# Two-layer decode: a third block of W_q kept, two heads projected earlier, unread MLP products left out

## The chip, the cores and the metric

The kernel runs on one core of a Trainium2 chip. The metric is the device time of one execution in microseconds, as the median of several runs. The same two layers' data are streamed from HBM in every run; nothing is kept between runs.

## What is computed

One token for each of 4 sequences goes through two identical layers, attention and a gated MLP, with the same weights and the same caches in both layers. All arrays are float32.

```
W = 1024                                  # last 1024 of 4096 cache rows, 32 heads of 128
x = x + A(layernorm(x)); x = x + M(layernorm(x))      # and the same once more

A(x): q = x @ wq                          # 640 -> 32 heads * 128
      p = softmax(q . k * 128**-0.5)      # over the last 1024 keys of each head
      return (p . v) @ wo                 # 4096 -> 640
M(x): gate = x @ W_gate; up = x @ W_up    # 640 -> 1728
      return (gate * (gate > 0) * up) @ W_down
```

## The kernel before

The inputs are laid out on the host in three long rows for each of 128 partitions. "heads" holds W_q, the keys, values and W_o of the groups of heads 0 to 6; "kept" holds W_o, W_q, keys and values of the last two groups, K0 and K1 (three and two heads), which layer 0 loads last and layer 1 uses first, so that they are loaded once; "mlp" holds W_gate, W_up and W_down. HEADS (L27) names the groups: six of four heads, then 3, 3 and 2.

Nearly all of SBUF is one tile, `store` (STORE columns), used as a ring, beside a small tile `first_q` (HELD columns), which holds the first HELD columns of "heads" for both layers. Those are the first blocks of W_q of the group 0, 512 columns each; the group has five. `load` (L156) takes the next piece of a list (L108 to L149), cuts it where it would run over live columns or over the ring's end, and issues it on SP's queue. `done` (L200) marks columns as read, frees them and calls `load`. So the moment at which a transfer can be issued is set by the product that read the columns it overwrites, and the order of the transfers by the list. FIRST and FIRST_MLP (L64) say where in the ring layer 0's heads and its MLP begin; at the ring's end the MLP of layer 0 goes on at FRONT = 47360, behind the kept columns. A load waits for one of eight completion semaphores as well, so that about eight are in flight.

An attention layer goes group by group: `query` (L310, products with W_q), `scores` (L338), `softmax`, `turned` (transposes of the probabilities), `values` (L360), `values_turned` (L388, transposes of the outputs `ot`, and VectorE's sums to `oT`) and `project` (L399), which adds a group's outputs times W_o to `y`. The last group's `values` is copied out by VectorE and ScalarE (L377, L378), each half the tile, and in layer 0 the projection of the last two groups follows behind `values_turned` of the last (L440 to L443).

`forward` (L445) is the MLP: four blocks of `gate`, then `down`. In layer 0 it also issues `busy` products (L254): transposes of the identity into `po`, which nothing reads. `busy` does something only while `waits[0]` is true: in every `normalized` (L270), and in layer 0's MLP behind its first gate block. A float32 product stands as two records in the trace, a transpose as one.

Of the kernel before, what the change touches and what calls it, by code (L numbers as in the profile page):

```python
# [13 lines left out]
P = 128  # L14
# [44 lines left out]

HELD = 1024  # L60
STORE = 54944 - HELD
QUARTERS = [STORE // 4, STORE // 2, STORE // 4 * 3, STORE]
FRONT = KEPT * 2 * (D + KV)
FIRST, FIRST_MLP = 10928, 53160  # L64

# [25 lines left out]
def decode_kernel(ctx: ExitStack, tc: tile.TileContext, x, source, sel, out):  # L91
# [162 lines left out]
    def busy(n):  # L254

        if waits[0]:
            for _ in range(n):
                nc.tensor.transpose(po[:, :P], ident, ident)  # L258


    waits = [False]

# [7 lines left out]
    def normalized():  # L270

        ysb, xc, sq = probs[:, :QUARTER], gates[:, :QUARTER], gates[:, QUARTER:2 * QUARTER]
        waits[0] = True
        su = small.tile([P, 1], F32, name="su", bufs=1)
# [123 lines left out]

    def project(layer, g, last=False):  # L399
        o = oT.pop(g)  # L400
        for i, h in enumerate(HEADS[g]):
            for a in range(4):
                nc.tensor.matmul(y[32 * a:32 * a + B], o[:, i], part(layer, "o", h, a * QUARTER, QUARTER),  # L403
                                 start=False, stop=last and h == HEADS[g][-1], tile_position=(0, 32 * a))
            part_done(layer, "o", h, 0, D)

    def attention(layer):
# [13 lines left out]
        for before, g, after, then in zip([None] + gs, gs, gs[1:] + [None], gs[2:] + [None] * 2):  # L421
# [15 lines left out]
            if before is not None and not (layer == 0 and after is None):  # L437
                project(layer, before)
            values(layer, g, after is None)
        values_turned(gs[-1])  # L440
        if layer == 0:
            project(layer, gs[-2])
        project(layer, gs[-1], True)  # L443

    def forward(layer):  # L445
# [4 lines left out]
        def gate(j):  # L450
# [3 lines left out]
            for c in range(KC):  # L454
                for g in range(groups):
                    lo = at + (c * groups + g) * 2 * n
                    nc.tensor.matmul(gus[j][32 * g:32 * g + 32, :2 * n], xT[:, B * c:B * c + 32], get(layer, "mlp", lo, 2 * n),  # L457
                                     start=c == 0, stop=c == KC - 1, tile_position=(0, 32 * g))
                    done(layer, "mlp", lo, 2 * n)
                if j == 2 or j == 1 and c > 2:  # L460
                    busy(2)
                if j == 3 and layer == 0 and c % 2:
                    load(True)
# [23 lines left out]
        def down(j, last=False):  # L487
            for f in range(4 if j < 3 else 1):
# [5 lines left out]
                done(layer, "mlp", lo, D)  # L494
                if not (last and f > 1):
                    busy(1)
            if j == 3:
# [7 lines left out]
        gate(3)  # L505
        waits[0] = layer == 0
        rstd = deviation(ss)
# [75 lines left out]
```

## Time and profile before

| | |
|---|---|
| median of 3 runs | 741.06 us (740.77 to 741.14) |
| the profiled execution's own time | 740.32 us |
| its span | 738.5 us |
| its mean granted TensorE clock | 0.829 |
| read from HBM | 312.24 MB, 423 GB/s over the span |
| PE busy | 453.3 us (61%) |
| DVE, ACT busy | 75.1 us (10%), 47.1 us (6%) |

The page's busy shares are averages over stages. Layer 0's attention runs to about 366 us, its MLP to 399, layer 1's attention to about 711, its MLP to the end. A window of the trace gives busy time, granted clock (1.00 is 2.4 GHz, 0.50 is 1.2 GHz) and the share of the 16 DMA engines that were moving something; the share can read a little over 1, since a packet's time is counted from its own start. The chain of waits is followed back from the last instruction: a transfer stands in it from issue to landing, whether it moves or queues.

### The profile page before, as it was taken

The page shows a single profiled execution, that of the slowest core. Times are in us where ns is not written, and L with a number is a line of the kernel's source. Part 1 is how long each engine was busy: PE and PEld are TensorE (multiplying, and loading weights), DVE is VectorE, ACT ScalarE, POOL GpSimd, SP SyncE. Part 2 cuts the span into 40 slices and gives each one's busy share as a digit, 9 for nine tenths or more (in the row PEclk, how much of TensorE's full clock was granted, in tenths as well). Part 3 has the DMA queues.
Part 4 walks back from the last instruction along what each step waited for, and adds up shares of the span by engine and source line. Part 5 has one row for each costly group of instructions (what it writes and reads, how often), then busy time and mean ns, then how long its engine had stood idle before and what let it go on. Part 6 is the DMA issues. An engine that isn't in the chain of part 4 may idle for free.

```text
span 738.5 us, 8243 instructions
## 1 busy us (share of the span) xinstructions
PE 453.3 (61%) x3749; PEld 143.2 (19%) x3749; DVE 75.1 (10%) x279; ACT 47.1 (6%) x88; POOL 0.2 (0%) x4
## 2 busy tenths in 40 slices
PE   1657366556567636726689898445756545656685
PEld 0111111011122201202333232101211111122242
DVE  1011000010001001101101211001010100001010
ACT  1100000000000000000101110000000000000110
POOL 0000000000000000000000000000000000000000
PEclk9889787867689867969999999867778977668899
DMA  9999999999999999999999999999999999999996
GB/s 393 448 409 439 441 425 428 447 417 431 441 431 424 426 446 411 445 418 420 410 397 394 427 430 427 443 427 446 425 431 423 447 426 425 438 434 427 422 423 281
DMA packets 15738, 312.85 MB, mean 424 GB/s; under 512 B 1748, under 2 KB 2260, under 8 KB 7512
## 3 DMA queue, kind: packets, MB, share of 16 engines
q1 hardware_dynamic: 15552, 312.24, 99.0%
q8 instruction: 29, 0.48, 0.3%
q10 hardware_dynamic: 152, 0.09, 0.0%
q14 instruction: 5, 0.04, 0.0%
HBM read 312.24 MB, written 0.08 MB: 423 GB/s over the span
## 4 chain that ended last, share of the span: by engine, by line
DMA 52%; PE 32%; another core or an unknown queue 14%; issue 1%; DVE 1%; ACT 0%; SPq 0%; DVEq 0%; ACTq 0%
DMA store<-in_heads 30%; PE ps L345 13%; DMA store<-in_mlp 12%; PE po L373 10%; DMA store<-in_kept 10%; PE qp L316 2%; PE pp L358 1%; PE y L403 1%; PE qp L321 1%; PE gu L457 1%; PE qt L333 1%; PE ot L393 0%; PE po L258 0%; PE so L384 0%
## 5 line engine op out<-in xcount | busy, mean ns | idle before, releaser
L345 PE MATMUL ps<-store,qT 128*4 128x512 f32 x1024 | 161.3, 700 | 106.2 <-DMA store<-in_heads 101.1
L373 PE MATMUL po<-store,pT 128*16 128x512 f32 x1024 | 155.9, 720 | 108.0 <-DMA store<-in_heads 97.4
L373 PEld LDWEIGHTS po<-store,pT 128*16 128x16 f32 x1024 | 34.7, 110 | 214.1 <-issue 131.0
L345 PEld LDWEIGHTS ps<-store,qT 128*4 128x4 f32 x1024 | 29.3, 93 | 220.1 <-DMA store<-in_heads 116.1
L349 DVE TENSOR_REDUCE nm<-ps 128x1 f32<-128x1024 f32 x18 | 22.0, 1225 | 243.4 <-PE ps L345 243.4
L353 ACT ACTIVATE probs<-ps,nm 128x1024 f32<-128x1024 f32 x18 | 20.0, 1113 | 353.3 <-DVE nm L349 345.6
L316 PE MATMUL qp<-store,xT 128*32 128x512 f32 (+2 forms) x136 | 23.6, 623 | 24.6 <-DMA store<-in_heads 24.5
L403 PE MATMUL y<-store,oT 128*4 128x160 f32 x512 | 26.0, 332 | 8.8 <-DMA store<-in_heads 7.6
L369 DVE COPY pT<-pp 128x16 f32<-128x16 f32 x128 | 17.1, 168 | 135.6 <-PE po L373 135.6
L457 PE MATMUL gu<-store,xT 128*32 128x256 f32 (+1 forms) x300 | 23.9, 379 | 9.1 <-DMA store<-in_mlp 8.6
L380 ACT COPY gates<-po 128x512 f32<-128x512 f32 x16 | 9.4, 586 | 244.3 <-PE po L373 244.3
L358 PE MATMUL pp<-sel_sb,probs 128*128 128x128 f32 x144 | 20.5, 289 | 0.0
L358 PEld LDWEIGHTS pp<-sel_sb,probs 128*128 128x128 f32 x144 | 18.1, 151 | 0.0
L321 PE MATMUL qp<-store,xT 128*32 128x512 f32 (+4 forms) x48 | 17.5, 512 | 0.0
L326 DVE TENSOR_SCALAR gates<-qp,rstd 128x512 f32<-128x512 f32 (+2 forms) x18 | 12.4, 690 | 49.9 <-PE qp L321 44.5
L386 DVE RECIPROCAL r<-so 128x16 f32<-128x16 f32 x18 | 4.6, 257 | 122.6 <-PE so L384 122.6
L403 PEld LDWEIGHTS y<-store,oT 128*4 128x4 f32 x512 | 13.3, 93 | 19.4 <-DMA store<-in_heads 8.2
L457 PEld LDWEIGHTS gu<-store,xT 128*32 128x32 f32 x300 | 11.0, 115 | 18.1 <-DMA store<-in_mlp 7.4
L492 PE MATMUL y<-store,hT 128*4 128x160 f32 x208 | 11.3, 329 | 3.4 <-DMA store<-in_mlp 3.2
L333 PE MATMUL qt<-sel_sb,gates 128*128 128x128 f32 x64 | 12.3, 316 | 0.0
L393 PE MATMUL ot<-sel_sb,gates 128*128 128x128 f32 x72 | 11.4, 279 | 1.2 <-DVE gates L377 1.2
L333 PEld LDWEIGHTS qt<-sel_sb,gates 128*128 128x128 f32 x64 | 7.6, 155 | 18.6 <-issue 17.3
(62 smaller groups left out, 108.5 us busy)
## 6 DMA issues: line engine op xcount, KB each, us to landing
store<-in_heads SPq DMA_DIRECT2D x18, 6656.0 KB, 54.2
store<-in_heads SPq DMA_DIRECT2D x7, 6912.0 KB, 52.2
store<-in_heads SPq DMA_DIRECT2D x2, 6592.0 KB, 54.6
store<-in_heads SPq DMA_DIRECT2D x2, 5376.0 KB, 65.5
store<-in_mlp SPq DMA_DIRECT2D x16, 640.0 KB, 6.9
store<-in_kept SPq DMA_DIRECT2D x4, 2048.0 KB, 40.4
store<-in_heads SPq DMA_DIRECT2D x3, 2560.0 KB, 20.9
store<-in_heads SPq DMA_DIRECT2D x1, 6896.0 KB, 46.1
```

What stands on the lines that cost most here:

```text
L316: nc.tensor.matmul(qp[g][32 * c:32 * c + 32, :], xT[:, B * c:B * c + 32], part(layer, "q", g, c * n, n), start=True, stop=c > 0 and not sp ...
L321: nc.tensor.matmul(qp[g][32 * a:32 * a + 32, a * m:a * m + m], xT[:, B * c:B * c + 32], part(layer, "q", g, c * n + a * m, m), start=False ...
L326: nc.vector.tensor_scalar(gates[:, :len(HEADS[g]) * P], qp.pop(g), rstd, SCALE, op0=ALU.mult, op1=ALU.mult)
L333: nc.tensor.transpose(qt[:, i], gates[:, i * P:(i + 1) * P], ident)
L345: nc.tensor.matmul(ps[32 * b:32 * b + SIDE, j, :], qT[:, at:at + SIDE], part(layer, "k", h, lo, 512), start=i == 0, stop=i == n - 1, tile_ ...
L349: nc.vector.tensor_reduce(nm[g], ps.rearrange("p j n -> p (j n)"), axis=AX.X, op=ALU.max, negate=True)
L353: nc.scalar.activation(probs, ps.rearrange("p j n -> p (j n)"), AF.Exp, bias=nm.pop(g), accum_out=sums[g])
L358: nc.tensor.transpose(pps[g][c // 4][:, c % 4, :], probs[:, c * P:(c + 1) * P], ident)
L369: nc.vector.tensor_copy(to[:, 4 * j:4 * j + 4], pp[j][:, :, i:P:32])
L373: nc.tensor.matmul(po[32 * a:32 * a + SIDE * B, :], t[:, at:at + SIDE * B], part(layer, "v", h, c * 512, 512), start=i == 0 and c < 4, sto ...
L403: nc.tensor.matmul(y[32 * a:32 * a + B], o[:, i], part(layer, "o", h, a * QUARTER, QUARTER), start=False, stop=last and h == HEADS[g][-1], ...
L457: nc.tensor.matmul(gus[j][32 * g:32 * g + 32, :2 * n], xT[:, B * c:B * c + 32], get(layer, "mlp", lo, 2 * n), start=c == 0, stop=c == KC - ...
```

## The change

HELD goes from 1024 to 1536, so a third 512-column block of W_q is loaded once for both layers; the store loses 512 columns, and FIRST and FIRST_MLP are moved. In layer 0 the first two heads of the last but one group are projected before the last outputs are transposed, the third behind it. `busy` no longer looks at `waits`, and its calls in the MLP are gone; those in `normalized` stay.

```diff
--- before.py
+++ after.py
@@ -57,11 +57,11 @@
 
 
 
-HELD = 1024
+HELD = 1536
 STORE = 54944 - HELD
 QUARTERS = [STORE // 4, STORE // 2, STORE // 4 * 3, STORE]
 FRONT = KEPT * 2 * (D + KV)
-FIRST, FIRST_MLP = 10928, 53160
+FIRST, FIRST_MLP = 9392, 50728
 
 
 def size_of(what, i):
@@ -253,12 +253,8 @@
 
     def busy(n):
 
-        if waits[0]:
-            for _ in range(n):
-                nc.tensor.transpose(po[:, :P], ident, ident)
-
-
-    waits = [False]
+        for _ in range(n):
+            nc.tensor.transpose(po[:, :P], ident, ident)
 
     def mean(a, name):
 
@@ -270,7 +266,6 @@
     def normalized():
 
         ysb, xc, sq = probs[:, :QUARTER], gates[:, :QUARTER], gates[:, QUARTER:2 * QUARTER]
-        waits[0] = True
         su = small.tile([P, 1], F32, name="su", bufs=1)
         nc.vector.tensor_reduce(su, y, axis=AX.X, op=ALU.add)
         nc.scalar.copy(ysb, y)
@@ -396,9 +391,9 @@
         nc.vector.tensor_reduce(oT[g], own, axis=AX.X, op=ALU.add)
         nc.vector.tensor_tensor(oT[g], oT[g], r.pop(g), op=ALU.mult)
 
-    def project(layer, g, last=False):
-        o = oT.pop(g)
-        for i, h in enumerate(HEADS[g]):
+    def project(layer, g, last=False, heads=slice(None)):
+        o = oT[g]
+        for i, h in list(enumerate(HEADS[g]))[heads]:
             for a in range(4):
                 nc.tensor.matmul(y[32 * a:32 * a + B], o[:, i], part(layer, "o", h, a * QUARTER, QUARTER),
                                  start=False, stop=last and h == HEADS[g][-1], tile_position=(0, 32 * a))
@@ -437,9 +432,11 @@
             if before is not None and not (layer == 0 and after is None):
                 project(layer, before)
             values(layer, g, after is None)
+        if layer == 0:
+            project(layer, gs[-2], heads=slice(2))
         values_turned(gs[-1])
         if layer == 0:
-            project(layer, gs[-2])
+            project(layer, gs[-2], heads=slice(2, None))
         project(layer, gs[-1], True)
 
     def forward(layer):
@@ -457,8 +454,6 @@
                     nc.tensor.matmul(gus[j][32 * g:32 * g + 32, :2 * n], xT[:, B * c:B * c + 32], get(layer, "mlp", lo, 2 * n),
                                      start=c == 0, stop=c == KC - 1, tile_position=(0, 32 * g))
                     done(layer, "mlp", lo, 2 * n)
-                if j == 2 or j == 1 and c > 2:
-                    busy(2)
                 if j == 3 and layer == 0 and c % 2:
                     load(True)
 
@@ -492,8 +487,6 @@
                     nc.tensor.matmul(y[32 * g:32 * g + B], hTs[j][:, f], w[:, g * QUARTER:(g + 1) * QUARTER],
                                      start=False, stop=last and f == 3, tile_position=(0, 32 * g))
                 done(layer, "mlp", lo, D)
-                if not (last and f > 1):
-                    busy(1)
             if j == 3:
                 w = get(layer, "mlp", TAIL, 2 * QUARTER)
                 for g in range(4):
@@ -503,7 +496,6 @@
                 done(layer, "mlp", TAIL, 2 * QUARTER)
 
         gate(3)
-        waits[0] = layer == 0
         rstd = deviation(ss)
         go_on()
         h = gated(3)
```

SP's queue where layer 0's MLP begins (a transfer's columns per partition; DMAHW are completions of earlier transfers, PE a product that must have run). Before:

```order
L185 DMA store<-in_kept 128x640 [waits DMAHW7_49]
L185 DMA store<-in_mlp 128x640 [waits DMAHW0_49]
L185 DMA store<-in_mlp 128x512 [waits DMAHW1_49]
L185 DMA store<-in_mlp 128x768 [waits DMAHW2_49]
L185 DMA store<-in_mlp 128x1280 [waits DMAHW3_49]
L185 DMA store<-in_mlp 128x1280 [waits DMAHW4_49]
L185 DMA store<-in_mlp 128x1280 [waits DMAHW5_49]
L185 DMA store<-in_mlp 128x512 [waits DMAHW6_49]
L185 DMA store<-in_mlp 128x768 [waits DMAHW7_49,DMAHW0_49,PE_49]
```

and now:

```order
L185 DMA store<-in_kept 128x640 [waits DMAHW7_49]
L185 DMA store<-in_mlp 128x1152 [waits DMAHW0_49]
L185 DMA store<-in_mlp 128x768 [waits DMAHW1_49]
L185 DMA store<-in_mlp 128x512 [waits DMAHW2_49]
L185 DMA store<-in_mlp 128x768 [waits DMAHW3_49]
L185 DMA store<-in_mlp 128x1280 [waits DMAHW4_49]
L185 DMA store<-in_mlp 128x1280 [waits DMAHW5_49]
L185 DMA store<-in_mlp 128x768 [waits DMAHW6_49,DMAHW0_49,PE_49]
```

Seven MLP transfers, 6272 columns, stood ahead of the first that waits for an MLP product; now six do, 5760 columns. Over the whole queue 107 loads became 108.

PE at the end of layer 0's attention (`po` the last group's values, `ot` the transposed outputs, `y` the projection). Before:

```order
L373 MATMUL po<-store,pT_98 16x512 x8
L373 MATMUL po<-store,pT_99 16x512 x8
L393 MATMUL ot<-sel_sb,gates 128x128 x4
L403 MATMUL y<-store,oT 4x160 x20
L258 MATMUL po<-sel_sb 128x128 x2
```

and now:

```order
L368 MATMUL po<-store,pT_98 16x512 x8
L368 MATMUL po<-store,pT_99 16x512 x8
L398 MATMUL y<-store,oT 4x160 x8
L388 MATMUL ot<-sel_sb,gates 128x128 x4
L398 MATMUL y<-store,oT 4x160 x12
L257 MATMUL po<-sel_sb 128x128 x2
```

Eight products, two heads of the group K0, stand ahead of the four transposes; twelve are left behind them.

PE in layer 0's MLP, from the second gate block on (`gu` gate and up products, `ph` a transpose, `po` the unread products). Before:

```order
L457 MATMUL gu<-store,xT 32x256 x16
L258 MATMUL po<-sel_sb 128x128 x2
L457 MATMUL gu<-store,xT 32x256 x4
L258 MATMUL po<-sel_sb 128x128 x2
L478 MATMUL ph<-sel_sb,gates 128x128
L457 MATMUL gu<-store,xT 32x256 x4
L258 MATMUL po<-sel_sb 128x128 x2
```

and now:

```order
L454 MATMUL gu<-store,xT 32x256 x20
L473 MATMUL ph<-sel_sb,gates 128x128
L454 MATMUL gu<-store,xT 32x256 x20
L473 MATMUL ph<-sel_sb,gates 128x128
L487 MATMUL y<-store,hT 4x160 x4
L494 MATMUL y<-store,hT 4x160 x4
L487 MATMUL y<-store,hT 4x160 x16
```

The gate products stand one behind the other; 14 unread products are gone from the gate blocks and 11 from `down`, and the products that remain keep their order.

## Rows read from the trace of the kernel before

**Rows 1.** The page: span, PE's busy time, SP's transfers (packets, MB, share).

```profile
span 738.5 us, 8243 instructions
...
PE 453.3 (61%) x3749; PEld 143.2 (19%) x3749; DVE 75.1 (10%) x279; ACT 47.1 (6%) x88; POOL 0.2 (0%) x4
...
q1 hardware_dynamic: 15552, 312.24, 99.0%
```

**Rows 2.** Windows: length, busy PE, PEld, DVE, ACT, POOL; clock, DMA share, GB/s.

```profile
184.00:244.00 60.00, 35.67 (x278) 10.06 (x270) 5.31 (x20) 3.00 (x5) 0.00 (x0) 0.81 0.99 429
372.00:400.00 28.00, 23.54 (x265) 8.94 (x260) 1.80 (x8) 1.39 (x4) 0.00 (x0) 1.00 1.01 396
...
728.00:732.00 4.00, 3.31 (x49) 1.39 (x49) 0.00 (x0) 0.00 (x0) 0.00 (x0) 0.66 0.89 362
732.00:736.00 4.00, 3.08 (x65) 1.39 (x65) 0.50 (x2) 0.00 (x0) 0.00 (x0) 0.91 0.26 98
```

**Rows 3.** Chain of waits: start, length, what; a transfer from issue to landing.

```profile
341.96 21.50 DMA store<-in_kept
...
363.48 9.64 DMA store<-in_mlp
...
390.99 6.05 DMA store<-in_mlp
...
403.86 5.38 PE ps L345 x48
...
712.18 22.84 DMA store<-in_mlp
```

**Rows 4.** DMA issues: tiles, queue, count, KB each, median us to landing.

```profile
store<-in_mlp SPq DMA_DIRECT2D x16, 640.0 KB, 6.9
...
first_q<-in_heads SPq DMA_DIRECT2D x1, 512.0 KB, 3.6
```

**Rows 5.** The unread products: their group of instructions, and two rows of the chain.

```profile
L258 PE MATMUL po<-sel_sb 128*128 128x128 f32 x37 | 10.1, 324 | 0.0
...
381.86 0.37 PE po L258 x2
...
389.94 0.26 PE po L258
```

**Rows 6.** Windows around layer 0's MLP, columns as in rows 2.

```profile
372.00:408.00 36.00, 31.16 (x353) 11.86 (x352) 3.68 (x14) 3.57 (x9) 0.00 (x0) 1.00 1.01 399
...
372.00:376.00 4.00, 2.88 (x34) 1.10 (x29) 0.19 (x2) 0.37 (x1) 0.00 (x0) 1.00 1.03 390
376.00:380.00 4.00, 2.44 (x28) 0.96 (x29) 0.24 (x1) 0.00 (x0) 0.00 (x0) 1.00 1.01 412
...
388.00:392.00 4.00, 3.87 (x49) 1.52 (x48) 0.43 (x2) 0.37 (x1) 0.00 (x0) 1.00 1.00 365
392.00:396.00 4.00, 3.67 (x54) 1.41 (x54) 0.17 (x1) 0.00 (x0) 0.00 (x0) 1.00 0.97 386
...
408.00:412.00 4.00, 1.73 (x15) 0.47 (x8) 1.32 (x2) 1.21 (x2) 0.00 (x0) 0.98 1.04 427
412.00:416.00 4.00, 4.00 (x25) 2.20 (x26) 0.26 (x1) 0.00 (x0) 0.00 (x0) 0.59 1.02 430
```

**Rows 7.** Timeline of PE, then of weight loads, at the end of layer 0's attention.

```profile
363.54 0.84 PE L393 MATMUL ot<-sel_sb,gates 128*128 128x128 f32 x4 [0.60 <-DVE gates L377]
...
364.32 2.07 PE L403 MATMUL y<-store,oT 128*4 128x160 f32 x40
...
365.10 0.38 PEld L403 LDWEIGHTS y<-store,oT 128*4 128x4 f32 x16 [0.40 <-DMA store<-in_kept]
365.93 0.11 PEld L403 LDWEIGHTS y<-store,oT 128*4 128x4 f32 x8 [0.45 <-DMA store<-in_kept]
```

**Rows 8.** Timeline of PE: sixteen value products at either level of the clock.

```profile
342.59 1.91 PE L373 MATMUL po<-store,pT 128*16 128x512 f32 x16 [0.69 <-DVE pT L369]
347.20 3.47 PE L373 MATMUL po<-store,pT 128*16 128x512 f32 x16 [2.70 <-DMA store<-in_kept]
```

## The prediction

> **What bounds the kernel now.** I read the page first. The transfers that SP issues carry 312.24 MB and take 99.0% of the span on all 16 DMA engines [rows 1]. That is 0.990 x 738.5 = 731.1 us of transfer in a span of 738.5 us; all the rest, the first issue and the end together, is 7.4 us. PE is busy 61% of the span [rows 1], so it can only matter where it comes too late to free room for the next transfer.
>
> Then the windows, to see what a byte costs. Where the transfers are large (184 to 244 us) the engines move 429 GB/s at a share of 0.99, which is 433 GB/s at a full share. In the MLP of layer 0, where they are cut small (372 to 400 us), it is 396 GB/s at 1.01, which is 392 [rows 2]. The share is full in both: the small pieces are slower, the queue isn't empty.
>
> Third, the chain of waits, for who releases whom. At the end of layer 0's attention a transfer of "kept" issued at 341.96 lands 21.5 us later. In the MLP the chain goes through single transfers that take 9.64 and 6.05 us from issue to landing. At the end the last MLP transfer, issued at 712.18, takes 22.84 and lands at 735.02; its products and the output follow [rows 3]. The chain puts this time down to transfers, but not whether it is moving or queueing, so I compare landings. The first transfer, 512 KB into an empty queue, lands after 3.6 us; at 433 GB/s 1.21 us of that is moving, so 2.4 us is fixed. A 640 KB piece of the MLP (655,360 bytes at 392 GB/s: 1.67 us) would land alone after 4.1 us. Its median is 6.9 us [rows 4] and the chain's shortest 6.05. So between 2.0 and 2.8 us of other transfers stood ahead of it: that is the **reserve** of the tightest stretch, by which PE can be later before the queue runs dry.
>
> **The change, part by part.**
>
> *The third block of W_q.* Layer 1 loads 512 columns fewer: 512 x 4 bytes x 128 partitions = 262,144 bytes. The queue never empties, so it is worth its transfer time: 0.605 us at 433 GB/s, 0.67 us at 392. I take 0.61, since all but the tight stretch runs at the higher rate.
>
> *The cuts.* The order of SP's queue shows 108 loads where there were 107; the extra one is a cut of the layer-0 MLP. What a cut costs is bounded by the two rates: 655,360 bytes take 1.51 us at 433 GB/s and 1.67 at 392, so a small piece costs up to 0.16 us more than its bytes. The lower end is 0, the upper end 0.3 if the whole 2.4 us of fixed latency were felt on one of eight pieces in flight. I take 0.15, the nearest row.
>
> By the Trainium skill (DMA: Bandwidth & Descriptors, Anatomy of one DMA), a DMA issued by GpSimd takes about 2.0 us plus its bytes at 436 GB/s; added to this sum instead of the 0.15, the change would end at plus 1.4 us. The rows speak against adding it here: pieces of at most 640 KB kept the share at 1.01 for 28 us [rows 2].
>
> *The shorter ring.* The store loses the same 512 columns. Where the MLP of layer 0 begins, seven transfers (6272 columns) could be issued before any MLP product had run; now it is six (5760), and the seventh waits for a gate product. The reserve shrinks by 0.61 us, to between 1.4 and 2.2 us. As long as it stays above zero this costs nothing; the upper bound is the full 0.61 us, were the queue to run dry once. What is late next if it does: the gate products behind that piece.
>
> *The 25 unread products.* Of 37 rows of this kind, 25 go, all of layer 0's MLP; the twelve of the four normalisations stay. On the chain a pair takes 0.37 us and a single one 0.26 us [rows 5]; seven pairs and eleven singles make 2.59 + 2.86 = 5.45 us of PE time. Beside it lies the stream: shares of 1.00 and 0.97 in the two windows from 388 to 396 us [rows 6]. PE frees the ring sooner, which gives back part of the lost reserve, but a transfer that is issued sooner only queues longer. The most it could return is what those two windows move less than the stage's mean: (365 + 386)/2 = 375.5 against 396 GB/s over 8 us, 0.41 us. I take 0: the share says that the engines are busy there with small pieces.
>
> *Two heads' projection.* Sixteen of the 40 records behind the output transposes now stand ahead of them, where PE sits idle 0.60 us until VectorE has copied; the loads of sixteen such products take 0.38 us [rows 7]. Behind the move PE still waits for the third and the fifth head's W_o, which land only at 365.10 and 365.93. These landings end the attention, so the move is worth 0. It adds a wait: the first piece of W_o must be there before the transposes. The second is used at 365.10; one 640 KB piece takes 1.67 us, so I estimate the first at about 363.4, against VectorE's 363.54, where the transposes start. The transposes may start some 0.3 us later, and the 0.4 us until 365.10 covers that; without the cover it would be 0.3 us on the way to the first gate product.
>
> *The end.* The last transfers are cut as before; nothing changes behind 735.02.
>
> **Sum:** -0.61 + 0.15 = -0.46 us. The profiled execution took 740.32, so 739.86 by its measure; the median of the runs shown is 741.06, 0.74 higher, so the **forecast is 740.6 us**. A measurement of this kernel can tell about 0.2% (1.48 us) from no change, so this is "same".
>
> **Rivals.**
>
> *The reserve runs dry.* The seventh MLP piece and those after it come too late, and the 0.61 us saved in layer 1 is lost in layer 0. For it: the piece now waits on PE. Against it: 1.4 us are left by the median row and the 25 products go. Result -0.46 + 0.61 = +0.15: 741.2 us, still "same".
>
> *The chain as it reads.* From 381.86 to 390.2 us the chain runs on PE through seven pairs and one single product, 7 x 0.37 + 0.26 = 2.85 us, and then into the transfer of 390.99. If the transfers really waited for PE there, all of it would come off: -0.46 - 2.85 = -3.3 us, 737.8 us. Against it: that transfer's 6.05 us holds 2 us of queue, and the share of the DMA engines has no hole of this size.
>
> *The clock falls* (the other side). The products stand where PE otherwise waits for pieces. The granted clock is 1.00 from 372 to 408 us; right after a stretch with 1.73 us of PE work in 4 it is 0.59, between the levels 1.2 and 2.4 GHz [rows 6]. Sixteen value products took 3.47 us after an idle 2.70 us and 1.91 us without it [rows 8], 1.82 times as long. If the clock went down at the change of layers, the 5.38 us of the first scores [rows 3] would take 9.8, 4.4 us more; the reserve covers 1.4 to 2.2, and some 2.6 us remain: 743.2 us. It decides from 1.4 us of lost PE time, that is from 1.7 us of work at the low clock. Against it: in 372 to 380 us there are no unread products, PE works 2.88 and 2.44 us of 4, and the clock stays at 1.00; the change makes 380 to 399 look like that. And the 0.59 window after 412 cost no share of the stream, 1.02.
>
> By the Trainium skill (TensorE: Matmul & The Clock Gate, What's actually happening), the low clock is the default and activity is what releases it, so taking products out speaks for this rival. The trace agrees on the direction only, by the 0.59 after 412.
>
> *A cut costs its fixed time in full.* One more transfer then adds about 2 us of the 2.4 us seen at the start: -0.61 + 2.0 = +1.4, 742.5 us. Against it: the full shares.
>
> **How the numbers follow.** Forecast 66%, reserve dry 15%, chain as it reads 9%, clock 7%, fixed cost 3%. The forecast's terms at their ends give 741.06 - 0.67 - 0.41 = 740.0 and 741.06 - 0.61 + 0.3 + 0.61 = 741.4. The runs shown spread by about 0.3 us to one side, which I add below and above; and the 16 engines do not finish together: shares of 0.89 and 0.26 in the last windows [rows 2] mean 0.44 + 1.98 = 2.4 us of mean idleness before 735.02, which can shift by some tenths with new cuts (nothing shows how much). I take 739.6 to 741.7; the three rivals outside hold 19%. Faster by over 0.2% (below 739.58): the chain's 9% and 2% of the forecast's edge, 0.11. Slower (above 742.54): clock and fixed cost, 0.10. Same: 0.79.
>
> **What would show it.** Right: SP's transfers carry 311.98 MB, their share stays at 99%, the granted clock is 1.00 from 372 to 408 us, PE idles for pieces where the products were, and W_o still lands last before the MLP. Wrong: a share below 0.95 between 366 and 376 us (reserve), a clock of 0.5 to 0.7 between 384 and 408 with a hole in the share behind it, or the first scores of layer 1 more than 1 us earlier and the end with them (chain).

## The result, and the profile after

| | before | change |
|---|---|---|
| median of 7 runs each | 740.77 us (740.49 to 741.14) | 743.43 us (742.30 to 745.81) |
| ratio | | 1.0039 [1.0025, 1.0053] |
| the profiled execution, its span | 740.32, 738.5 us | 744.51, 742.6 us |

The change is slower by 2.7 us, 0.39%, where 740.6 us and no measurable difference were forecast, against a median of 741.06 then known: wrong in direction, and outside the range. The time is that of the rival "the clock falls" (743.2 us, given 7%), but two thirds of the loss remain in a run whose clock stays up, as shown below.

The page of the change, in the lines of [rows 1]:

```profile
span 742.6 us, 8195 instructions
...
PE 455.9 (61%) x3724; PEld 143.0 (19%) x3724; DVE 75.3 (10%) x279; ACT 47.1 (6%) x88; POOL 0.2 (0%) x4
...
q1 hardware_dynamic: 15696, 311.97, 98.7%
```

The transfers carry 0.27 MB less, as planned. PE does 25 instructions less, yet is busy 2.6 us longer: what is left takes longer. That sum does not lead to the place: PE is busy 2.8 us longer from 424 to 700 us alone, where the stream's rate is the same.

To find the place I cut the span into stages and read what the stream moved in each. First before, then the change, columns as in [rows 2]; the last is GB/s:

```profile
340.00:366.00 26.00, 17.17 (x169) 5.51 (x165) 3.70 (x17) 3.65 (x6) 0.00 (x0) 0.93 1.01 418
366.00:388.00 22.00, 17.75 (x199) 7.62 (x199) 2.13 (x9) 2.03 (x7) 0.00 (x0) 1.00 1.01 399
388.00:408.00 20.00, 18.39 (x237) 7.25 (x240) 2.81 (x10) 2.83 (x7) 0.00 (x0) 1.00 1.01 397
408.00:424.00 16.00, 12.66 (x93) 4.47 (x89) 4.36 (x12) 2.41 (x4) 0.00 (x0) 0.89 1.02 428
424.00:700.00 276.00, 171.44 (x1291) 51.63 (x1287) 25.73 (x99) 14.60 (x24) 0.00 (x0) 0.80 1.00 431
```

```profile
340.00:366.00 26.00, 17.11 (x171) 5.92 (x165) 3.71 (x17) 3.65 (x6) 0.00 (x0) 0.93 1.00 418
366.00:388.00 22.00, 15.80 (x187) 6.82 (x179) 2.19 (x9) 2.03 (x7) 0.00 (x0) 1.00 0.99 381
388.00:408.00 20.00, 15.23 (x183) 6.21 (x183) 2.27 (x8) 2.84 (x7) 0.00 (x0) 0.66 0.93 345
408.00:424.00 16.00, 13.70 (x103) 3.70 (x102) 2.93 (x6) 1.21 (x2) 0.00 (x0) 0.89 1.00 393
424.00:700.00 276.00, 174.26 (x1280) 50.24 (x1280) 27.03 (x101) 14.15 (x24) 0.00 (x0) 0.81 1.00 431
```

From 340 to 366 us and from 424 to 700 the rates are equal. Between them the change moves 18 GB/s less for 22 us, 52 less for 20 us and 35 less for 16 us: 0.40 + 1.04 + 0.56 = 2.0 MB, which is 4.6 us at 433 GB/s. The spans differ by 4.1 us, and 0.6 us of bytes were saved, together 4.7. The whole loss lies in layer 0's MLP and the change of layers. Two things are to be seen in it. Up to 388 us the clock is 1.00 and the DMA share 0.99, and still the rate is down: **the share of busy engines hardly shows this loss**. Even at the start of the stretch, before and then the change, the share falls by 4% and the rate by 9%:

```profile
368.00:376.00 8.00, 6.19 (x96) 3.29 (x89) 0.81 (x5) 0.94 (x3) 0.00 (x0) 1.00 1.01 388
```

```profile
368.00:376.00 8.00, 6.49 (x91) 3.28 (x88) 0.80 (x5) 0.94 (x3) 0.00 (x0) 1.00 0.97 354
```

Behind 388 the clock is low as well.

The chain of waits of the change, start, length, what:

```profile
342.77 23.05 DMA store<-in_kept
...
370.71 5.65 DMA store<-in_mlp
...
377.15 6.28 DMA store<-in_mlp
...
385.11 6.17 DMA store<-in_mlp
...
391.83 7.38 DMA store<-in_mlp
...
399.35 2.31 PE y L487 x32
...
408.27 5.38 PE ps L340 x48
```

Between transfers the chain no longer runs through pairs of unread products as in [rows 5]; it goes from transfer to transfer, four of 5.65 to 7.38 us with less than 2 us of PE's work between them. Its 32 down products at 399.35 take 2.31 us, and layer 1's first scores start at 408.27 instead of 403.86 [rows 3]. Those scores themselves take 5.38 us in both: at that point the clock is back.

PE's timeline of the change shows where it fell (start, length, then in brackets the idle time before and its releaser):

```profile
391.33 1.28 PE L487 MATMUL y<-store,hT 128*4 128x160 f32 x24 [0.99 <-DMA store<-in_mlp]
394.51 0.72 PE L487 MATMUL y<-store,hT 128*4 128x160 f32 x8 [1.90 <-DMA store<-in_mlp]
...
396.09 1.25 PE L487 MATMUL y<-store,hT 128*4 128x160 f32 x16 [0.46 <-DMA store<-in_mlp]
397.70 1.25 PE L487 MATMUL y<-store,hT 128*4 128x160 f32 x16 [0.36 <-DMA store<-in_mlp]
399.35 2.31 PE L487 MATMUL y<-store,hT 128*4 128x160 f32 x32 [0.40 <-DMA store<-in_mlp]
```

PE waits 0.99 and then 1.90 us for pieces, and behind the second wait the same products take 0.72 us for eight, 1.25 for sixteen. Before, eight took 0.46 us behind idle times of 0.22 and 0.66 us, as two rows of its timeline show:

```profile
395.16 0.45 PE L492 MATMUL y<-store,hT 128*4 128x160 f32 x8 [0.22 <-DMA store<-in_mlp]
397.18 0.46 PE L492 MATMUL y<-store,hT 128*4 128x160 f32 x8 [0.66 <-DMA store<-in_mlp]
```

The granted clock by stretches:

```profile
391.00:394.50 3.50, 1.18 (x24) 0.43 (x24) 0.00 (x0) 0.00 (x0) 0.00 (x0) 0.88 1.00 370
394.50:402.00 7.50, 6.28 (x75) 2.32 (x75) 0.45 (x2) 0.00 (x0) 0.00 (x0) 0.50 0.91 332
402.00:408.00 6.00, 5.69 (x59) 2.72 (x57) 1.33 (x5) 2.47 (x6) 0.00 (x0) 0.56 0.90 325
```

From 394.5 to 402 it is 0.50, the level of 1.2 GHz; PE is busy 84% of that stretch, and the stream falls to 332 GB/s at a share of 0.91. Up to 399 us PE still waits for pieces, 0.36 to 0.46 us each. Then it is the stream that waits: the longest wait of SP, which issues the loads, from 394 to 408 us is 3.8 us for a product of layer 1's queries, and was 2.5 us before.

### The profile page after: what moved, and what is told of

Read it like the earlier page. It is cut to its first block, busy times and chain, and to the rows that moved or that the text cites. A ratio compares the mean times of both kernels' runs of the same rounds, so it can differ in the third digit from the quotient of the medians.

```text
span 742.6 us, 8195 instructions
## 1 busy us (share of the span) xinstructions
PE 455.9 (61%) x3724; PEld 143.0 (19%) x3724; DVE 75.3 (10%) x279; ACT 47.1 (6%) x88; POOL 0.2 (0%) x4
## 4 chain that ended last, share of the span: by engine, by line
DMA 45%; PE 36%; another core or an unknown queue 16%; issue 1%; DVE 1%; ACT 0%; SPq 0%; DVEq 0%; ACTq 0%
DMA store<-in_heads 24%; PE ps L340 14%; DMA store<-in_mlp 13%; PE po L368 12%; DMA store<-in_kept 9%; PE y L398 2%; PE qp L311 2%; PE pp L353 1%; PE qp L316 1%; PE qt L328 1%; PE gu L454 1%; PE ot L388 1%; PE y L487 0%; PE so L379 0%
## 5 line engine op out<-in xcount | busy, mean ns | idle before, releaser
L340 PE MATMUL ps<-store,qT 128*4 128x512 f32 x1024 | 165.4, 716 | 106.8 <-DMA store<-in_heads 102.4
L368 PEld LDWEIGHTS po<-store,pT 128*16 128x16 f32 x1024 | 37.0, 111 | 192.0 <-issue 102.5
L311 PE MATMUL qp<-store,xT 128*32 128x512 f32 (+2 forms) x132 | 25.5, 678 | 22.1 <-DMA store<-in_heads 21.9
L316 PE MATMUL qp<-store,xT 128*32 128x512 f32 (+4 forms) x48 | 19.6, 572 | 0.0
```

Of the source, the lines that this page charges most:

```text
L311: nc.tensor.matmul(qp[g][32 * c:32 * c + 32, :], xT[:, B * c:B * c + 32], part(layer, "q", g, c * n, n), start=True, stop=c > 0 and not sp ...
L316: nc.tensor.matmul(qp[g][32 * a:32 * a + 32, a * m:a * m + m], xT[:, B * c:B * c + 32], part(layer, "q", g, c * n + a * m, m), start=False ...
L340: nc.tensor.matmul(ps[32 * b:32 * b + SIDE, j, :], qT[:, at:at + SIDE], part(layer, "k", h, lo, 512), start=i == 0, stop=i == n - 1, tile_ ...
L368: nc.tensor.matmul(po[32 * a:32 * a + SIDE * B, :], t[:, at:at + SIDE * B], part(layer, "v", h, c * 512, 512), start=i == 0 and c < 4, sto ...
```

## The experiments

Each median stands beside the median of before from runs on the same chip, and each ratio with its 95% interval. "Loss by windows" is what a run moved less than before in 366 to 424 us, at 433 GB/s, worked out as above from the rows of 366:388, 388:408 and 408:424 in its profile.

### The parts of the change

**e1_products_back**: the change, with its 25 unread products put back.

```diff
+                if layer == 0 and (j == 2 or j == 1 and c > 2):
+                    busy(2)
...
+                if layer == 0 and not (last and f > 1):
+                    busy(1)
```

> The changed kernel with the 25 unread products of layer 0's MLP put back; the third block of W_q and the earlier projection stay. Three theories for the 2.7 us: the clock falls because the products are gone (C), the shorter ring lets the queue run dry (R), the earlier projection holds the transposes up (P). C: 740.3 us, the 0.46 us of the forecast below the 740.8 of before, and a clock of 1.00 from 372 to 408 us. R and P: still about 743.4 us.

Measured: 742.59 us against 740.81, 1.0023 [1.0014, 1.0032]. Two thirds of the loss are still there with all the products in place. The clock is 1.00 up to 408 us:

```profile
366.00:388.00 22.00, 16.73 (x191) 7.36 (x191) 2.12 (x9) 2.02 (x7) 0.00 (x0) 1.00 0.98 371
388.00:408.00 20.00, 17.98 (x230) 7.13 (x232) 2.81 (x10) 2.84 (x7) 0.00 (x0) 1.00 1.00 373
408.00:424.00 16.00, 12.66 (x93) 3.76 (x89) 4.01 (x10) 2.19 (x3) 0.00 (x0) 0.89 1.02 428
```

Its loss by windows is 0.62 + 0.48 = 1.09 MB, 2.5 us; the spans (740.6 and 738.5) and the saved bytes ask for 2.1 + 0.6 = 2.7. So there is a loss at a full clock.

**e2_products_out**: before, without the 25 products (both calls of `busy` in the MLP taken out).

```diff
-                if j == 2 or j == 1 and c > 2:
-                    busy(2)
...
-                if not (last and f > 1):
-                    busy(1)
```

> The kernel before with nothing but the 25 unread products taken out. C: 743 to 744 us, a spread of some us between runs as with the change, a clock of about 0.5 somewhere between 390 and 408 us and a DMA share below 0.95 there. R and P: 740.8 us, unchanged.

Measured: 741.15 us against 740.81, 1.0008 [0.9998, 1.0017]; runs from 740.43 to 743.76. On the long ring the products are worth 0.3 us, an amount that can't be told from nothing, though single runs lose some 3 us. In its profile the clock is 0.91 in 388 to 408 us and the stream holds 392 GB/s, then 409 from 408 to 424, where before has 428.

**e3_third_block**: before, with the third block and the change's ring alone.

```diff
-HELD = 1024
+HELD = 1536
-FIRST, FIRST_MLP = 10928, 53160
+FIRST, FIRST_MLP = 9392, 50728
```

> The kernel before with the third block of W_q held and the store 512 columns shorter, products and projection as before. C and P: 740.3 us (-0.61 for the block, +0.15 for one more cut). R: about 743.4 us, with a low DMA share from 368 to 376 us.

Measured: 742.27 us against 740.81, 1.0022 [1.0013, 1.0031]. The part that was to bring the gain costs 1.5 us by itself, at a clock of 1.00 up to 408 us.

**e4_two_heads**: before, with the split projection alone.

```diff
+        if layer == 0:
+            project(layer, gs[-2], heads=slice(2))
         values_turned(gs[-1])
         if layer == 0:
-            project(layer, gs[-2])
+            project(layer, gs[-2], heads=slice(2, None))
```

> The kernel before with the projection of two heads moved ahead of the last transposes, nothing else. C and R: 740.8 us, unchanged, since W_o's last pieces end the attention anyway. P: above 742 us, with the transposes starting more than 0.5 us after 363.5.

Measured: 740.87 us against 740.81, 1.0000 [0.9991, 1.0008]. Nothing, as predicted.

### The ring's length

**e5_short_ring**: before, with 512 columns of the store left unused and the MLP cut as in the change. No byte is saved; the ring is shorter, and with it the cuts and the place of the pieces are others.

```diff
-STORE = 54944 - HELD
+STORE = 54944 - HELD - 512
-FIRST, FIRST_MLP = 10928, 53160
+FIRST, FIRST_MLP = 8880, 50728
```

> The kernel before, two blocks of W_q held as before, but with a store that is 512 columns shorter; the cuts of layer 0's MLP are then those of the change, six transfers ahead of the first gate product. The space theory (the ring lost the columns that the held block takes, so the DMA engines run dry at the MLP's start): the 1.5 us that the third block cost plus the 0.5 us that it saved, about 742.8 us, with 368 to 376 us at about 350 GB/s. The rival (something in the held block itself, its product or its tile, costs the time): 740.8 to 741.0 us.

Measured: 742.85 us against 740.81, 1.0027 [1.0017, 1.0037]. The shorter ring costs 2.0 us. With the saved bytes that makes e3: 2.0 - 0.6 = 1.4, against 1.5 measured. Its windows:

```profile
366.00:388.00 22.00, 16.81 (x194) 7.46 (x197) 2.12 (x9) 2.03 (x7) 0.00 (x0) 1.00 0.99 372
388.00:408.00 20.00, 17.58 (x228) 7.05 (x232) 2.81 (x10) 2.83 (x7) 0.00 (x0) 1.00 1.00 382
```

Clock 1.00, shares 0.99 and 1.00, and 27 and 15 GB/s missing. To somebody who reads shares nothing in these two rows would have looked like a stall.

The issue times of the transfers show what the ring does. Layer 0's MLP goes round in the columns from FRONT to the end of the store: 6560 of them before, 6048 here, where a 640 KB piece takes 1280. Counted from the landing of the last W_o piece, the transfer that brings column 9000 of the MLP's 25920 is issued after 5.32 us in before, 6.32 in the change, 6.36 in e3, 6.46 here and 6.29 in e15, which has only 256 columns less. So the transfers come about 1.0 us later, not 0.61. Layer 1's first load, which overwrites columns of the MLP too, is late as well: issued at 394.07 us in before, at 395.92 in e3, 396.06 in e1, 396.85 in the change and 396.92 here. How the loss behind 388 us divides between that load and the pieces ahead of it, and how the whole divides between the ring's length, its cuts and the place of the pieces, no run separates.

**e6_long_ring**: the other way, HELD = 512 and a ring of 512 columns more; layer 1 loads 0.26 MB more.

```diff
-HELD = 1024
+HELD = 512
-FIRST, FIRST_MLP = 10928, 53160
+FIRST, FIRST_MLP = 12464, 53160
```

> The kernel before with one block of W_q held instead of two, and the store 512 columns longer; 6784 columns of the MLP stand ahead of the first gate product. The space theory: 0.61 us more to load, and fewer dry engines, between 740.2 and 741.0 us, with 368 to 376 us above 388 GB/s. The rival (space does not matter, bytes do): 741.4 us.

Measured: 743.01 us against 740.81, 1.0032 [1.0020, 1.0044], a miss. The profile shows a hole that before has not:

```profile
392.00:396.00 4.00, 3.56 (x48) 1.32 (x49) 0.17 (x1) 0.00 (x0) 0.00 (x0) 1.00 0.98 378
396.00:400.00 4.00, 3.58 (x55) 1.53 (x54) 0.43 (x2) 0.29 (x1) 0.00 (x0) 1.00 0.67 203
```

With FIRST_MLP unchanged, layer 1's first load came to lie on columns that a later product reads, and was issued at 397.51 us instead of 394.07. The run tests the placement, not the length.

**e10_long_ring_2**: the same with the MLP placed so that this load falls on columns read earlier; the diff is against e6.

```diff
-FIRST, FIRST_MLP = 12464, 53160
+FIRST, FIRST_MLP = 12464, 49280
```

> One block of W_q held and the store 512 columns longer, as in the long ring tried first, but with the MLP put at another column, so that the first load of layer 1 falls on columns that are read early, where the first long ring left a hole of 1.5 us at 392 to 400. The space theory: 0.61 us more bytes against fewer dry engines, 740.2 to 741.0 us, without that hole. The rival (a longer ring gives nothing back): 741.4 us or more.

Measured: 741.18 us against 740.70, 1.0007 [0.9998, 1.0015]. The hole is gone; what is left, 0.5 us, is about its 0.6 us of additional bytes. A longer ring gives nothing back that this run can tell.

**e15_ring_256** and **e16_ring_768**: before, with 256 and 768 columns left unused.

```diff
-STORE = 54944 - HELD
+STORE = 54944 - HELD - 256
-FIRST, FIRST_MLP = 10928, 53160
+FIRST, FIRST_MLP = 10128, 52096
```

```diff
-STORE = 54944 - HELD
+STORE = 54944 - HELD - 768
-FIRST, FIRST_MLP = 10928, 53160
+FIRST, FIRST_MLP = 8080, 49792
```

> The kernel before with a store only 256 columns shorter, products as before, two more cuts. The space theory (the queue's depth all through the stretch sets how often a DMA engine runs dry, with a steep rise below the depth of before): between before and the 742.85 us of 512 columns, about 741.6. A rival (a threshold between 256 and 512): 741.1 us, the cuts alone.

> The kernel before with a store 768 columns shorter, products as before. The space theory: worse than 512 columns, 743.3 to 744.5 us. The rival (the cost of a thin queue is capped at the time of the missing columns, 1.5 times 0.61 us): at most 741.9 us.

Measured: 742.40 us, 1.0026 [1.0015, 1.0037], and 745.90 us, 1.0070 [1.0050, 1.0090], both against 740.58. So 256, 512 and 768 columns cost 1.8, 2.0 and 5.3 us. The loss is not capped at the 0.61 us by which 512 columns are shorter, and it is not proportional either: e15 was expected at 741.6 and costs as much as e5. The issue times under e5 go with that: with their cuts, e15's transfers come nearly as late as e5's.

### A late PE on the long ring

**e9_late_start**: before, with five unread products ahead of layer 0's first gate block, meant to let PE begin the MLP 0.7 us later, once.

```diff
+        if layer == 0:
+            busy(5)
         gate(3)
```

> The kernel before, its ring and loads untouched, with five more unread products on PE right ahead of layer 0's first gate block; they make it start about 0.7 us later. The reserve theory (0.6 us less of queued transfers when the first gate product runs costs some 2 us): 742.3 to 742.9 us, with 368 to 376 us at about 350 GB/s and the clock still at 1.00 until 408 us. The rival (a share near 1 means that such a delay is hidden): 740.8 us.

Measured: 740.76 us against 740.70, 0.9999 [0.9990, 1.0008]. A miss: I had expected 742.3 to 742.9. The eighth transfer is issued at 369.80 us instead of 369.07, and nothing comes of it. But the run tested less than it was meant to. The first gate product, in before and then in e9 behind the projection:

```profile
368.39 1.18 PE L457 MATMUL gu<-store,xT 128*32 128x128 f32 x27 [0.30 <-DVE xT L289]
```

```profile
364.79 2.01 PE L403 MATMUL y<-store,oT 128*4 128x160 f32 x40
...
369.13 1.18 PE L457 MATMUL gu<-store,xT 128*32 128x128 f32 x27
```

In e9's profile the projection already runs 0.47 us later than in [rows 7], the seventh transfer, which waits for no MLP product, is issued 0.46 us later, and the five products fill an idle stretch of 0.30 us. Against the landing of the last W_o piece PE is only 0.33 us late. The transfer that brings column 9000 is 0.32 us late, that of column 10000 not at all. So a delay of 0.3 us at the start is absorbed; one of 0.61 us or more was not tested.

**e11_late_down**: before, with each unread down product three times: 22 more, 5.7 us of PE's work spread over the down block.

```diff
-                    busy(1)
+                    busy(3)
```

> The kernel before with three unread products instead of one behind each W_down piece of layer 0, 22 more, some 5.7 us of PE time between 389 and 399 us at a clock of 1.00. The reserve theory: PE falls behind by more than the 2.0 to 2.8 us in reserve there, so 742 to 744 us with a low share from 396 to 408. The rival (only the clock matters there): 740.8 us.

Measured: 742.05 us against 740.70, 1.0015 [1.0007, 1.0024]. At a clock of 1.00, more work on PE alone costs 1.35 us on the long ring. The stream in 388 to 408 us:

```profile
388.00:408.00 20.00, 19.51 (x248) 9.02 (x252) 2.81 (x10) 2.83 (x7) 0.00 (x0) 1.00 1.00 382
```

It is 15 GB/s below before, the same 382 and the same share of 1.00 as e5 there, from the other side: PE later instead of the ring shorter.

**e12_other_start**: before, with the MLP's beginning put elsewhere, the ring's length the same.

```diff
-FIRST, FIRST_MLP = 10928, 53160
+FIRST, FIRST_MLP = 10928, 53504
```

> The kernel before with layer 0's MLP put at column 53504 of the store instead of 53160: the same bytes and the same ring, 768 columns more ahead of the first gate product, two more cuts. The reserve theory: fewer dry engines against 0.3 us for the cuts, 740.3 to 740.9 us. The rival: 741.1 us, the cuts alone.

Measured: 740.70 us against 740.70, 0.9999 [0.9990, 1.0008]. Not every placement matters.

### The unread products on the short ring

**e7_down_only** and **e8_gate_only**: the change, with the eleven products of the down block, or with the fourteen of the gate blocks: the first addition below is e7's, the second e8's.

```diff
+                if layer == 0 and not (last and f > 1):
+                    busy(1)
```

```diff
+                if layer == 0 and (j == 2 or j == 1 and c > 2):
+                    busy(2)
```

> The changed kernel with the 11 unread products behind the W_down pieces put back, and not the 14 in the gate blocks. The clock theory (with the short ring, PE's low clock at the end of the MLP drains the queue): they lie where the clock fell, so about 742.5 us as with all 25, and a clock of 1.00 from 392 to 404 us. The rival (the products matter as work or as delay, wherever they stand): halfway, 743.0 us, or as the change, 743.4.

> The changed kernel with the 14 unread products in the gate blocks put back, and not the 11 behind the W_down pieces. The clock theory: the clock still falls between 392 and 408 us and the time stays near 743.4 us. The rival: 743.0 us or, if the gate blocks are where the products are needed, 742.5.

Measured, both against 740.81: 744.10 us, 1.0044 [1.0027, 1.0061], and 743.96 us, 1.0045 [1.0032, 1.0057]. Neither half helps, and neither kept the clock up. PE's timeline of e7:

```profile
394.74 0.45 PE L487 MATMUL y<-store,hT 128*4 128x160 f32 x8 [1.47 <-DMA store<-in_mlp]
396.33 0.71 PE L487 MATMUL y<-store,hT 128*4 128x160 f32 x8 [0.23 <-DMA store<-in_mlp]
```

and of e8:

```profile
397.27 0.73 PE L489 MATMUL y<-store,hT 128*4 128x160 f32 x16 [0.85 <-DMA store<-in_mlp]
399.45 2.31 PE L489 MATMUL y<-store,hT 128*4 128x160 f32 x32 [1.46 <-DMA store<-in_mlp]
```

In each, PE waits almost 1.5 us for a piece. In e8 the products behind that wait are slow, 2.31 us for 32 where sixteen took 0.73. In e7 they are not: eight take 0.45 us right behind the wait of 1.47, and 0.71 from 396.33 us on, behind one of 0.23.

**e13_more_products**: the change, with 41 products: a pair behind every step of the gate blocks 0 to 2, and the eleven of the down block.

```diff
+                if layer == 0 and j < 3:
+                    busy(2)
...
+                if layer == 0 and not (last and f > 1):
+                    busy(1)
```

> The changed kernel with unread products behind every step of its three large gate blocks and behind the W_down pieces of layer 0, 41 of them, 16 more than before had. The clock theory (a low clock before 408 us costs the change some 1 us on top of the ring's 1.8): the clock stays at 1.00 from 372 to 408 us and the time comes back to 742.3 to 742.9 us. The rival (the products have no part in it): 743.4 us or more, as the change.

Measured: 743.15 us against 740.58, 1.0030 [1.0018, 1.0042]. The clock stays at 1.00, and the stream is slower still, 361 GB/s in 366 to 388 us and 366 in 388 to 408. More products hold the clock and delay PE: no way out on this ring.

**e14_short_no_products**: e5's ring, without the 25 products; beside e5's lines:

```diff
-                if j == 2 or j == 1 and c > 2:
-                    busy(2)
...
-                if not (last and f > 1):
-                    busy(1)
```

> The short ring alone (two blocks held, 512 columns fewer, 742.85 us) with the 25 unread products taken out; no third block, projection as before. The clock theory: the clock falls between 390 and 408 us, and 743.5 to 744.3 us. The rival (the products have no part in it): 742.8 us.

Measured: 744.34 us against 740.58, 1.0052 [1.0039, 1.0065], where e5 has [1.0017, 1.0037]. On the short ring taking the products out costs 1.5 us, with intervals that don't touch; on the long ring (e2) 0.3. Its PE timeline shows the change's picture again, idle 1.84 us and then slow:

```profile
390.80 1.28 PE L490 MATMUL y<-store,hT 128*4 128x160 f32 x24 [0.71 <-DMA store<-in_mlp]
393.92 0.71 PE L490 MATMUL y<-store,hT 128*4 128x160 f32 x8 [1.84 <-DMA store<-in_mlp]
395.51 1.25 PE L490 MATMUL y<-store,hT 128*4 128x160 f32 x16 [0.47 <-DMA store<-in_mlp]
```

The execution that was profiled took 742.32 us, the fastest of its five. In it the clock is 0.83 in 388 to 408 us, and yet the stream moves 382 GB/s there, as in e5 at 1.00: in this trace the low clock costs nothing. The other four took 744.28 to 745.27 us; that the clock is what they lost by is not shown.

## Why the prediction was wrong

**The sum, term by term, as measured.** The bytes: forecast -0.61 with +0.15 for a cut; e3 against e5 gives 1.46 - 2.04 = -0.6, and e10 pays 0.5 for the same bytes the other way. Both lie within the intervals of these runs, and nothing speaks against this step; the cut's 0.15 is not seen in e12, which has two more and loses nothing. The two heads' projection: forecast 0, measured 0.06 with an interval around 0 (e4). Right; W_o still lands last before the MLP, as the chain's "kept" transfer at 342.77 and its eight products show. The ring: forecast 0, at most 0.61; measured +2.0 (e5). Wrong. The products: forecast 0; measured +0.8 on the change's ring (743.43 - 742.59, intervals overlapping) and +1.5 on e5's (apart). Wrong. Put together, -0.6 + 2.0 + 0.8 = 2.2, or 2.9 with 1.5, around the 2.7 that the change lost. A slip in the chances changes nothing here: "fixed cost" at 742.5 was counted as above 742.54.

**The step that failed first** is "As long as it stays above zero this costs nothing; the upper bound is the full 0.61 us, were the queue to run dry once." What the order had shown came true: the seventh MLP transfer waits for a gate product and is issued at 369.01 us instead of 365.07. But the lateness was mis-sized: the transfers behind it come about 1.0 us later, as the issue times under e5 show, not 0.61. And the reserve, by the forecast's own measure, never went to zero. The group of the 640 KB pieces in the pages of e1, e5 and e15:

```profile
store<-in_mlp SPq DMA_DIRECT2D x14, 640.0 KB, 6.3
```

```profile
store<-in_mlp SPq DMA_DIRECT2D x14, 640.0 KB, 6.5
```

```profile
store<-in_mlp SPq DMA_DIRECT2D x14, 640.0 KB, 7.0
```

From issue to landing the median was 6.9 us [rows 4]; the change's own is 6.8, and e15 lost 1.8 us with a median that had not fallen. The shortest such piece issued behind 365 us took 5.97 us in before, 5.80 in the change, 5.72 in e5 and 5.57 in e15, all above the 4.1 us that the forecast gave a piece alone. A reserve of about 1.5 us or more was left by that measure, and still the ring cost 2 us. So the sentence on what the reserve covers is wrong, and in two ways.

The first is to treat the reserve as one number. I let a median stand for the whole queue, and let it be a store that is either there or empty. It is not: with 512 columns less the rate in 366 to 388 us went from 399 to 371 to 381 GB/s while the share stayed at 0.98 to 1.00 (e1, e3, e5 and the change). The sign that I had named for this rival, a share below 0.95 from 366 to 376 us, did not come either: 0.97 in 368 to 376. The likeliest reading is that the 16 engines are not level. Then the engines that are ahead would run out of pieces and take up the next one late, while those behind still move. In the packets' own records, which no view of the profile groups, I count in 360 to 440 us the packets of 1 KB or more that took over 150 ns longer than their size takes at 27 GB/s, a sixteenth of 433: 49 in before and 105 to 145 in e3, e1 and the change, 1.3 us per engine before and 2.9 to 3.7 after. That agrees with it, but e4, whose median is that of before and whose profiled span is 0.8 us longer, has 87. Why a packet takes longer when its engine has run dry, and which engine is ahead, is not shown.

The second is "once". A shorter ring makes issue after issue later: in e5 the transfers that bring columns 8000, 9000 and 10000 come 0.9, 1.1 and 1.3 us later than in before. In e9 the delay was 0.3 us, ended by column 10000 and cost nothing; the shorter rings cost 1.8, 2.0 and 5.3 us for 256, 512 and 768 columns. A single delay of the ring's own size was not tested, so that the repetition is what costs is argued. It is also why I priced the rival "the reserve runs dry" at 0.61 us and with it at "same". Its direction was right and its size wrong: the ring costs 2.0 us (e5), not 0.61.

The sign that would have told was in [rows 2]. I read 396 GB/s at a share of 1.01 as "the small pieces are slower, the queue isn't empty", that is as a property of the pieces. It is partly that: e10, with the longer ring, moves no more (389 and 402). But pieces of the same size at a share of 0.99 to 1.00 move 372 to 382 in e5. A rate that is already below that of the other stages, at a share that can't show why, was no ground for a bound.

**The second step that failed** is "I take 0" for the products, and with it the argument against the clock. It went: from 372 to 380 us there are no unread products, PE is busy 2.88 and 2.44 us of 4, and the clock holds; the change makes 380 to 399 look like that. It does not: from 391 to 394.5 us PE is busy 1.18 us of 3.5. With the products gone and the pieces late, PE runs up to the stream and waits for it in longer stretches: 0.99, then 1.90 us, where before the waits of the down block were 0.22 and 0.66. The average share of PE over long stretches is what I compared, and waits are what the rows show ahead of every fall of the clock: the last one is 1.90 us in the change, 1.84 in e14, 1.47 and then 0.23 in e7, and e8 has five of 0.35 to 1.46. A single wait does not decide, as a row of e3, whose clock stays at 1.00 up to 408 us, and one of e2 show:

```profile
392.21 0.45 PE L492 MATMUL y<-store,hT 128*4 128x160 f32 x8 [1.26 <-DMA store<-in_mlp]
```

```profile
397.14 1.18 PE L490 MATMUL y<-store,hT 128*4 128x160 f32 x24 [0.95 <-DMA store<-in_mlp]
```

In e2 no wait of the down block is longer than that 0.95 us, and still the clock is 0.64 from 400 to 404 us. In sum, the waits over 0.2 us from 386 to 400 us come to 5.6 us in the change and 5.4 in e2, against 0.9 in before. How much waiting it takes is not shown.

By the Trainium skill (TensorE: Matmul & The Clock Gate, What's actually happening) the low clock is the default and activity releases it. I had granted that the trace agrees "on the direction only"; the change agrees in that the clock falls, to 0.50 from 394.5 us, where PE has waited.

The rival itself was right in kind and in its sign (a clock of 0.5 with a hole in the share behind it, 0.91), wrong in its place: I put the slow work on the first scores, which take 5.38 us after as before. What is slow is the down block and layer 1's first queries; 32 products take 2.31 us in the chain where sixteen took 0.73 before. That its 743.2 us is close to the 743.43 measured is mostly luck: two thirds of the loss come from the ring.

**The two parts need each other.** Products out on the long ring: +0.3, nothing that can be told. Products out on the short ring: +0.8 to +1.5. In e2 PE waits as much in all as in the change, but in pieces of at most 0.95 us, and its clock falls only behind the down block, for a shorter time: 0.91 against 0.66 from 388 to 408 us. That the long ring also leaves the stream some depth while PE is slow is likely, and not shown. I priced each part alone, against a reserve that the other was using up.

**What remains open.** Why eleven or fourteen products don't hold the clock where 25 do: e8 lacks those of the down block, where its waits lie, but e7 has them and falls all the same. How much of the ring's 2.0 us is length, and how much cuts and place. What the low clock costs: in the change's profile 3.7 us are lost by windows behind 388 us, in e1's 1.1, but the medians differ by 0.8 only, and e14's profile shows a low clock at no loss. Whether the loss by windows is all: in the change, e1, e3, e5, e7, e13 and e14 it agrees with the spans to 0.3 us or better, but e2, e8 and e15 show some 0.6 us less than their spans, e16 2.6 of 3.4 us, and e11 only 0.8 of 2.0. No version was found that beats before; e4, e9 and e12 equal it.

## What to carry to other kernels

Here the rate of a stream fell when the ring that feeds it became shorter, while the share of busy DMA engines hardly moved: compare GB/s by stage, and do not take the spare time of a median transfer as a reserve that costs nothing until it is gone. Columns that are kept for reuse are paid from that depth; here 0.6 us of saved bytes cost 2.0 us of rate. Look up what the ring is where it is tightest, 6560 columns here and not the whole store, and how late each transfer is issued. And work that nobody reads may be holding something up: before it goes, look at the waits that it fills, each and in sum, together with the other parts of the change, rather than at the engine's mean share over a long stretch.

## What was not expected of the hardware

The same MLP data, with the share of the 16 DMA engines at 0.97 to 1.01, moved between 361 (e13) and 399 GB/s (before) in 366 to 388 us; I had taken a share of 1 for a full stream. The granted clock was 1.00 up to 391 us with PE busy 13.54 us of the 20 from 372 to 392, and 0.50 from 394.5, behind waits of 0.96, 0.51, 0.99 and 1.90 us; it stayed there until 402 although PE was then busy 6.28 us of 7.5, and was back to 1.00 from 408:

```profile
372.00:392.00 20.00, 13.54 (x148) 4.82 (x143) 1.41 (x6) 1.10 (x3) 0.00 (x0) 1.00 1.00 384
...
404.00:408.00 4.00, 3.99 (x31) 1.85 (x31) 0.78 (x2) 1.63 (x3) 0.00 (x0) 0.58 0.91 345
408.00:412.00 4.00, 3.97 (x38) 0.97 (x41) 0.60 (x2) 0.00 (x0) 0.00 (x0) 1.00 1.02 401
```
